# A build-time list scheduler for the order of all instructions, a variable share of exps on VectorE, and the last sums in two jobs

## The chip, the cores and the metric

The kernel runs on one core of a Trainium2 chip. The metric is the time of one execution in device microseconds (us). A run is given as the median of its executions; the span of a profile is the time from the first to the last instruction of the one execution that was profiled. PE is the matmul engine, ACT the engine of activation functions, DVE the vector engine, POOL and SP are the two others. PEld is PE's loading of weights, which overlaps its matmuls (5 us of the trace below, from 555.00, hold 4.58 us of PE and 1.36 of PEld).

## The reference

Two independent parts share one output of 2048 x 1024. Part A is attention with 32 heads of 16 dimensions and one common key and value; part B is linear attention with a softmax feature map.

```python
q = (x @ wq).reshape(B, S, 32, 16)           # part A, S = 2048
k, v = x @ wk, x @ wv                        # one key and value for all heads
p = softmax(einsum("bhqd,bkd->bhqk", q, k) * 16 ** -0.5)
a = einsum("bhqk,bkd->bhqd", p, v) @ wo

pq, pk = q2 @ w_phi, k2 @ w_phi              # part B, per head
phi = concat(softmax(pq), softmax(-pq))      # the same for k
kv, z = phi_k.T @ v2, phi_k.sum(0)
b = ((phi_q @ kv) / (phi_q @ z + 1e-6)) @ wo2
```

Part A has 32 x 2048 x 2048 exps. The kernel cuts them into 2048 score tiles of 128 keys by 512 queries. That is nearly all of the work outside PE.

## The kernel before

The head dimension is only 16, padded to 32, so a score matmul uses 32 rows of the array, and up to four of them run side by side on four row groups. The trace of the kernel before shows it: three score matmuls start together at 506.88 us, within 0.01 us, and the next job starts 0.32 us after them; four start at 507.75 us, and the next job 0.34 us after. Each product with the values uses 32 columns, again four side by side: four start at 506.13 us, and the next four 0.22 us later.

ACT takes exps in groups of three and two tiles, out of five PSUM banks used in turn (3 + 2). One bank collects the products with the values. The last two banks, 6 and 7, serve everything else: projections, all of part B, and the score tiles whose exp DVE computes from integer bits. In the kernel before, the order was written by hand. Each step emits one score group and its exp, then whatever is due, up to a budget of PE time; what is left of the budget is filled with matmuls by zero ("fills"), which are meant to keep PE's clock up (in the runs below the clock was 0.784 to 0.808 without them and 0.873 to 0.898 with those of the changed kernel).

```python
def misc(self):                               # the two shared banks, in turn
    b = self.MISC[self.misc_n % len(self.MISC)]
    self.misc_n += 1
    return b

def d_unit(self, busy):                       # one score tile for DVE
    ...
    bank = self.misc()
    self.add("pe", lambda pe: self.score(pe, bank, sc, kap, g), cost=0.1, ...)
    o = self.Z[:, p, h, :]
    self.add("dve", lambda v: v.tensor_scalar(out=o, in0=ps[:, bank, :], scalar1=self.Z1, scalar2=self.Z0, op0=ALU.mult, op1=ALU.add), ...)
    if h:
        self.d_fields(k // 2)                 # two bit operations on a pair of tiles
    self.d_mul(k // 2 - 1 + h, 1 - h)         # two multiplications on a pair

self.layout([0] + [3, 2] * 15 + [0])          # quads of tiles on DVE, for each 512 queries of four heads: 75 in all
...
for i, (n0, size, b0) in enumerate(gs):       # plan()
    self.pe_used = over
    self.qk(n0, size, b0)
    self.expo(n0, size, b0)
    ...                                       # a DVE tile, and products with V, if due
    budget = self.EXP_US[gs[i - 1][1]] if i else 0.5
    while H and H[0][0] <= i:                 # projections, part B: by due step
        if self.pe_used > budget and H[0][0] > i - 5 and i > 12:
            break
        heapq.heappop(H)[2]()
    if i >= 13 and self.open:
        ...
        while self.pe_used + 0.216 <= budget:
            self.fill()
```

Each engine is given its instructions in this order. A semaphore holds each one until its inputs and its buffers are ready, and the timeline below shows what that does to those behind it (a score matmul waited 1.58 us for DVE at 563.67 us).

## Time and profile before

The time before was 1070.84 us (median of 2 runs, 1068.35 to 1073.33).

| | before |
|---|---|
| span of the profile | 1069.9 us |
| busy: PE, ACT, DVE | 81%, 79%, 72% |
| ACT idle for score matmuls | 207.0 us |
| mean granted clock | 0.868 |
| filling matmuls recorded | 493 |
| score tiles on ACT, on DVE | 1748, 300 |

The first fence has lines of the profile page of the kernel before: the busy time of each engine; the granted clock of PE in 40 slices of the span, in tenths; the chain of waits that ended last; and four groups of instructions. A group has line, engine, operation and shapes, then busy us and mean ns of one, then the idle time of the engine just before them and what ended most of it. L1441 is the exps on ACT, L1421 the score matmuls, L1479 the first DVE step of a DVE tile, L1256 the fills.

```profile
PE 870.9 (81%) x6933; PEld 248.0 (23%) x6933; DVE 771.3 (72%) x1401; ACT 846.3 (79%) x768; POOL 16.5 (2%) x44
PEclk9899898989986989698987888969789688988998
...
DVE 35%; PE 32%; ACT 25%; DMA 3%; SPq 2%; issue 1%; DVEq 0%; POOL 0%; POOLq 0%
...
L1441 ACT ACTIVATE f_PT<-f_ps 128x1536 bf16<-128x1536 f32 (+1 forms) x699 | 816.7, 1277 | 209.2 <-PE f_ps L1421 207.0
L1421 PE MATMUL f_ps<-f_QA,f_KR 32*128 32x512 bf16 x2048 | 331.5, 421 | 109.1 <-ACT f_PT L1441 58.7
L1479 DVE TENSOR_SCALAR f_Z<-f_ps 128x512 int16<-128x512 f32 x300 | 205.1, 684 | 120.4 <-PE f_ps L1421 120.2
...
L1256 PE MATMUL f_ps<-f_ones,f_zero 128*128 128x512 bf16 x493 | 166.8, 417 | 1.9 <-POOL f_zero L1280 1.3
```

No engine is full. ACT waits for scores, and DVE waits for scores too. The next fence, from the table of windows of the kernel before, shows one episode: us, then busy us of PE, PEld, DVE, ACT and POOL, then the granted clock, DMA share and GB/s.

```profile
555.00:560.00 5.00, 4.58 (x38) 1.36 (x36) 3.95 (x8) 4.29 (x4) 0.00 (x0) 1.00 0.00 0
560.00:565.00 5.00, 3.19 (x30) 0.92 (x28) 4.90 (x9) 3.28 (x3) 0.00 (x0) 1.00 0.08 30
565.00:570.00 5.00, 1.96 (x19) 0.86 (x19) 4.93 (x12) 1.66 (x2) 0.00 (x0) 0.52 0.10 28
570.00:575.00 5.00, 3.94 (x12) 1.06 (x13) 2.20 (x4) 0.82 (x1) 0.00 (x0) 0.50 0.00 0
575.00:580.00 5.00, 3.69 (x34) 0.91 (x36) 2.65 (x5) 3.87 (x4) 0.00 (x0) 0.84 0.00 0
```

DVE is full from 560 to 570, PE is half idle, the clock falls to 0.50, and ACT does 0.82 us of work in 5. The timeline of the kernel before shows why PE is idle: the brackets give the idle time before an instruction and what ended it.

```profile
563.67 0.39 PE L1421 MATMUL f_ps<-f_QA,f_KR 32*128 32x512 bf16 x1 [1.58 <-DVE f_outA L1267]
564.27 0.40 PE L1808 MATMUL f_ps<-f_ident,f_o_sb 128*128 128x128 bf16 x4 [0.21 <-DVE f_Z L1479]
...
566.86 0.60 PE L1421 MATMUL f_ps<-f_QA,f_KR 32*128 32x512 bf16 x1 [1.87 <-DVE f_Z L1479]
...
568.39 0.38 PE L1785 MATMUL f_ps<-f_Zc,f_pT 128*128 128x4 bf16 x8 [0.93 <-DVE f_Z L1479]
...
569.79 1.02 ACT L1441 ACTIVATE f_PT<-f_ps 128x1024 bf16<-128x1024 f32 x1 [3.31 <-PE f_ps L1421]
...
572.09 3.68 PE L1574 MATMUL f_ps<-f_wo_pad,f_On 128*128 128x512 bf16 x8
...
576.13 4.62 ACT L1441 ACTIVATE f_PT<-f_ps 128x1536 bf16<-128x1536 f32 x4 [5.32 <-PE f_ps L1421]
```

A score tile for DVE, or a job of part B (L1808, L1785), stands in PE's queue, waits for one of the two shared banks, and everything behind it waits too, the scores for ACT among them. The last two lines show a second loss: the hand-written order put the eight matmuls of an output projection before the next scores. PE is busy with them, but at half clock they take 3.68 us (eight of the same line took 2.13 us at full clock, from 283.89 us), and ACT has waited 5.32 us when the scores come.

### The profile page before, as it was taken

How to read it: one execution, taken by the hardware profiler on the slowest of the kernel's cores; microseconds unless marked ns; L12 is line 12 of the kernel's file. 1: busy time of each engine (PE TensorE's matmuls, PEld its weight loads, DVE VectorE, ACT ScalarE, POOL GpSimd, SP SyncE). 2: the span in 40 equal slices, each digit the busy share in tenths (PEclk: the TensorE clock that was granted, in tenths of full speed). 3: DMA queues.
4: the chain of work that ended last, by engine and by line, in shares of the span. 5: the costliest groups of instructions: out<-in, count | busy, mean ns of one | idle time of the engine just before them, and what ended most of it. 6: DMA issues, size and time to landing. Idle time of an engine off the chain costs nothing.

```text
span 1069.9 us, 16576 instructions
## 1 busy us (share of the span) xinstructions
PE 870.9 (81%) x6933; PEld 248.0 (23%) x6933; DVE 771.3 (72%) x1401; ACT 846.3 (79%) x768; POOL 16.5 (2%) x44
## 2 busy tenths in 40 slices
PE   8897888888777879788796888888778788887885
PEld 2222222222221212122221222222122122222221
DVE  4577679778676887777857877787776787878712
ACT  5889787988866978688874888969778578877994
POOL 4000000000000000001000000000000000000000
PEclk9899898989986989698987888969789688988998
DMA  6700010000001000000000100111000010011110
GB/s 119 159 7 6 6 7 6 4 4 6 6 12 17 5 6 7 6 1 6 6 6 11 17 6 6 6 26 6 1 6 6 31 16 6 6 26 6 7 25 23
DMA packets 40667, 17.06 MB, mean 16 GB/s; under 512 B 32580, under 2 KB 38212, under 8 KB 40584
## 3 DMA queue, kind: packets, MB, share of 16 engines
q1 hardware_dynamic: 40584, 15.93, 12.0%
q8 instruction: 55, 0.90, 0.4%
q14 instruction: 28, 0.23, 0.1%
HBM read 3.19 MB, written 4.19 MB: 7 GB/s over the span
## 4 chain that ended last, share of the span: by engine, by line
DVE 35%; PE 32%; ACT 25%; DMA 3%; SPq 2%; issue 1%; DVEq 0%; POOL 0%; POOLq 0%
ACT f_PT L1441 23%; PE f_ps L1421 10%; DVE f_Z L1479 9%; DVE f_C L1501 7%; PE f_ps L1454 5%; PE f_ps L1256 4%; PE f_ps L1394 3%; DVE f_phi L1727 3%; DVE f_U L1489 3%; DVE f_ssum L1719 3%; PE f_ps L1515 2%; DVE f_E L1491 2%; ACT f_epn L1713 2%; PE f_ps L1574 2%; DMA f_denS<-f_denS 2%; PE f_ps L1676 2%
## 5 line engine op out<-in xcount | busy, mean ns | idle before, releaser
L1441 ACT ACTIVATE f_PT<-f_ps 128x1536 bf16<-128x1536 f32 (+1 forms) x699 | 816.7, 1277 | 209.2 <-PE f_ps L1421 207.0
L1421 PE MATMUL f_ps<-f_QA,f_KR 32*128 32x512 bf16 x2048 | 331.5, 421 | 109.1 <-ACT f_PT L1441 58.7
L1479 DVE TENSOR_SCALAR f_Z<-f_ps 128x512 int16<-128x512 f32 x300 | 205.1, 684 | 120.4 <-PE f_ps L1421 120.2
L1454 PE MATMUL f_ps<-f_PT,f_VA 128*32 128x512 bf16 x1748 | 170.7, 426 | 17.4 <-DVE f_accS L1267 15.9
L1256 PE MATMUL f_ps<-f_ones,f_zero 128*128 128x512 bf16 x493 | 166.8, 417 | 1.9 <-POOL f_zero L1280 1.3
L1421 PEld LDWEIGHTS f_ps<-f_QA,f_KR 32*128 32x128 bf16 x2048 | 73.3, 92 | 398.0 <-ACT f_PT L1441 244.2
L1501 DVE TENSOR_TENSOR f_C<-f_Z,f_U 128x1024 f16<-128x1024 f16 x150 | 102.7, 684 | 0.0
L1501 DVE TENSOR_TENSOR f_C<-f_C,f_U 128x1024 f16<-128x1024 f16 x150 | 102.1, 680 | 0.0
L1489 DVE TENSOR_SCALAR f_U<-f_Z 128x1024 int16<-128x1024 int16 x150 | 64.1, 427 | 5.2
L1491 DVE TENSOR_SCALAR f_E<-f_Z 128x1024 int16<-128x1024 int16 x150 | 63.0, 420 | 0.0
L1454 PEld LDWEIGHTS f_ps<-f_PT,f_VA 128*32 128x32 bf16 x1748 | 36.8, 97 | 106.8 <-issue 69.2
L1559 DVE TENSOR_TENSOR f_On<-f_accS,f_denS 128x512 bf16<-128x512 f32 x31 | 21.3, 689 | 51.9 <-DMA f_denS<-f_denS 51.9
L1256 PEld LDWEIGHTS f_ps<-f_ones,f_zero 128*128 128x128 bf16 x493 | 38.0, 100 | 87.1 <-issue 68.3
L1394 PE MATMUL f_ps<-f_AxT,f_wq_pad 128*128 128x512 bf16 x128 | 47.0, 506 | 13.6 <-DVE f_Z L1479 12.4
L1727 DVE TENSOR_TENSOR f_phi<-f_epn,f_rs 128x1024 bf16<-128x1024 f32 x32 | 39.2, 1224 | 1.1
L1676 PE MATMUL f_ps<-f_BxT,f_Bw 128*128 128x512 bf16 x128 | 37.3, 419 | 2.7 <-DVE f_Z L1479 2.0
L1719 DVE TENSOR_REDUCE f_ssum<-f_epn 128x64 f32<-128x1024 f32 x32 | 38.6, 1207 | 0.0
L1267 DVE CAST f_QA<-f_ps 128x512 bf16<-128x512 f32 x32 | 22.0, 688 | 21.6 <-PE f_ps L1394 21.5
L1713 ACT ACTIVATE f_epn<-f_ps 128x512 f32<-128x512 f32 x64 | 35.7, 633 | 1.2 <-PE f_ps L1704 1.2
L1574 PE MATMUL f_ps<-f_wo_pad,f_On 128*128 128x512 bf16 x96 | 31.3, 459 | 5.4 <-ACT f_epn L1713 1.9
L1515 PE MATMUL f_ps<-f_E,f_VK 128*32 128x512 f16 x300 | 32.6, 425 | 0.0
L1515 PE MATMUL f_ps<-f_Z,f_VK 128*32 128x512 f16 x300 | 32.1, 419 | 0.0
(90 smaller groups left out, 462.0 us busy)
## 6 DMA issues: line engine op xcount, KB each, us to landing
f_denS<-f_denS SPq DMA_DIRECT2D x124, 30.0 KB, 3.1
out_dram<-f_outB SPq DMA_DIRECT2D x4, 512.0 KB, 3.4
f_denC<-f_accS SPq DMA_DIRECT2D x124, 2.0 KB, 1.7
f_denS<-f_denC SPq DMA_DIRECT2D x124, 2.0 KB, 1.7
f_Bw<-in_B_wqkv_dram SPq DMA_DIRECT2D x1, 1536.0 KB, 8.0
out_dram<-f_outA SPq DMA_DIRECT2D x6, 256.0 KB, 2.6
f_outB<-in_A_wq_dram SPq DMA_DIRECT2D x1, 512.0 KB, 4.4
f_Bwo<-in_B_wo_dram SPq DMA_DIRECT2D x1, 512.0 KB, 7.8
```

Source lines behind the costliest of these rows:

```text
L1256: mm = pe.matmul(out, lhsT=self.zero, rhs=rhs, start=start, stop=start)
L1394: mm = pe.matmul(ps[:, bank, :], lhsT=self.wq_pad[:, dc, a, :], rhs=xT[:, dc, qc * 512:(qc + 1) * 512], start=(dc == 0), stop=(dc == 3))
L1421: return pe.matmul(self.ps[:, bank, :], lhsT=self.KR[32 * g:32 * g + 32, kap * 128:(kap + 1) * 128], rhs=self.QA[32 * g:32 * g + 32, sc % ...
L1441: self.add("act", lambda a: a.activation(out=PT[:, sl[0]:sl[0] + size, :], in_=ps[:, b0:b0 + size, :], func=ACT.Exp), reads=[("PS", b0 + i ...
L1454: mm = pe.matmul(ps[32 * g:32 * g + 32, bank, :], lhsT=VA[:, kap, :], rhs=PT[:, slots[g], :], start=start, stop=stop, tile_position=(0, 32 ...
L1479: self.add("dve", lambda v: v.tensor_scalar(out=o, in0=ps[:, bank, :], scalar1=self.Z1, scalar2=self.Z0, op0=ALU.mult, op1=ALU.add), reads ...
L1489: self.add("dve", lambda v: v.tensor_scalar(out=U, in0=Z, scalar1=0x3ff, scalar2=0x3c00, op0=ALU.bitwise_and, op1=ALU.bitwise_or), reads=z ...
L1491: self.add("dve", lambda v: v.tensor_scalar(out=E, in0=Z, scalar1=0x7c00, scalar2=None, op0=ALU.bitwise_and), reads=zk, writes=[("E", p)])
L1501: self.add("dve", lambda v: v.tensor_tensor(out=C, in0=a, in1=U, op=ALU.mult), reads=rd + [("U", r)], writes=[("C0", p), ("C", p)] if h == ...
L1515: mm = pe.matmul(ps[32 * g:32 * g + 32, bank, :], lhsT=self.VK[:, k, kap, :], rhs=terms[k][:, p, h, :], start=start and k == 0, stop=stop ...
L1719: self.add("dve", lambda v: v.tensor_reduce(out=ssum[:, r, :], in_=epn[:, r, :, :].rearrange("p a (h f) -> p (a h) f", h=32), axis=AX.X, o ...
L1727: self.add("dve", lambda g: g.tensor_tensor(out=o, in0=i0, in1=i1, op=ALU.mult), reads=[("epn", r), ("epn2", r), ("rs", r)], writes=[("phi ...
```

## The change

The change replaces the hand-written steps by jobs with a length, an engine and a list of what must come first. A list scheduler runs a model of the engines at build time. On each engine it picks, among the jobs whose inputs and banks the model says are ready, the one with the best priority; on PE, a job that uses the array in the same tiling as the job before has a bonus. Banks are named at that moment, the one that frees first. PE is held free when a job would delay the next score group (`spare`). Fills go into planned gaps when PE's busy time over the last 3.4 us of the model is below 80%. Which tiles DVE takes is decided on the way, from DVE's load. The final sums of part B put numerator and denominator into one bank and go in two halves. The arithmetic of the result is otherwise the same. The core of the diff, with cuts marked and some lines joined:

```diff
-    def misc(self):
-        b = self.MISC[self.misc_n % len(self.MISC)]
-        self.misc_n += 1
-        return b
+    def ready(self, j):                       # (cut) the latest of its inputs in the model,
+        ...                                   # and of the banks it needs:
+        if j.nb:
+            fr = sorted(max(self.tr.get(("PS", b), (0.0,))[0], 0.0) + self.SEM for b in self.free)
+            if len(fr) < j.nb:
+                return None
+            t = max(t, fr[j.nb - 1])
+        return t
+    def active(self, t, win=3.4):
+        while self.pe_hist and self.pe_hist[0][1] < t - win:
+            self.pe_hist.pop(0)
+        return sum(min(b, t) - max(a, t - win) for a, b in self.pe_hist) / win
 ...
-        self.layout([0] + [3, 2] * 15 + [0])
-        for i, (n0, size, b0) in enumerate(gs):
-            ...
+    def dq_ok(self):                          # may DVE take another tile?
+        if self.dbusy > 3.2 or self.dz_out or (...):
+            return False
+        return self.dn % 4 != 0 or self.dve_quad() is not None
+    def run(self):
+        while True:
+            ...
+                lo = min(o[0] for o in opts)
+                now = [o for o in opts if o[0] <= max(lo, te) + 0.02]
+                if eng == "pe":
+                    now = self.spare(now, opts)
+                s, j = min(now, key=lambda o: (self.rank(o), o[1].seq))
+            ...
+            if j.eng == "pe" and self.open:
+                te = self.te["pe"]
+                if s - te > 0.36 and te > 14 and self.active(te) < self.ACTIVE:   # ACTIVE = 0.80
+                    n = min(int((s - te - 0.12) / 0.216), 4)
+                    self.issue(_Job(("fill", len(self.log)), "pe", 0.216 * n, lambda: self.fill(n), ...), te)
+                    continue
 ...
-            for G in range(8):
-                mm = pe.matmul(ps[:, bd, 4 * G:4 * G + 4], lhsT=pT[:, r, G, :], rhs=Zc[:, G, :], start=True, stop=True)
-            for G in range(8):
-                mm = pe.matmul(ps[:, bn, 64 * G:64 * G + 64], lhsT=pT[:, r, G, :], rhs=KV[:, G, :], start=True, stop=True)
+            for i in range(4):                # twice per row tile: h = 0, 1
+                mm = pe.matmul(ps[:, bank, 68 * i:68 * i + 68], lhsT=pT[:, r, 4 * h + i, :], rhs=KVZ[:, 4 * h + i, :], start=True, stop=True)
```

## The prediction

> **What bounds the kernel now.** No engine is full: PE is busy 81%, ACT 79%, DVE 72% of 1069.9 us (busy time by engine). The chain of waits is shared: DVE 35%, PE 32%, ACT 25%. ACT's exps (the groups) take 816.7 us for 1748 of the 2048 score tiles, 0.467 us a tile; ACT's idle time is almost all one wait, 207 us for score matmuls. Those come late because PE takes instructions in order and stands behind a matmul whose PSUM bank DVE has not emptied (waits of score matmuls for DVE f_Z, f_o_sb, f_outA, f_kvS; at 564-575 us of the timeline). DVE in turn idles 120 us before f_Z, waiting for scores. So the fixed order passes stalls round a loop.
>
> The rest of the loss is the clock. Of 5-us windows after 20 us, 116 with full clock show ACT 94% busy, 31 with clock at most 0.6 show 53%, 52 between show 67%. Mean granted clock is 0.868; with cold at 0.5 that is 26% of the time cold. Cold stretches follow windows in which DVE is full (4.9 of 5 us) and PE stalls.[...]
>
> **What the change does.** It keeps nearly all arithmetic. It orders jobs by modelled readiness, so that PE should not queue behind an unready bank, reserves room for the next score group, picks the bank that frees first, and fills PE only when its recent activity is below 80%. Part B's last sums go in two halves with numerator and denominator in one bank: 8 matmuls a row tile instead of 16, one bank at a time instead of two (that wait costs PE about 12 us now)[...]. DVE's share of exps becomes dynamic; I expect it to rise from 300 to 330-420 tiles.
>
> **Cost.** A DVE tile occupies about 1.55 us: steps in the timeline are 0.60 for f_Z, half of 0.34+0.34 and of 0.60+0.60 per pair. DVE's other work is 234 us busy, about 215 occupied (estimate). ACT has about 30 us of other work, 12 us before its first exp, 12 us of tail. The last 60 us have DVE nearly idle; a dynamic share can use that. With ACT useful 94% and DVE 86%: (0.94T-40)/0.467 + (0.86T-215)/1.55 = 2048 gives T = 885 us (estimate); full use about 830. PE, without most of its 167 us of fills, has some 700 us of work when warm (estimate), so it is no bound unless cold.
>
> Prediction: **885 us**, 840 to 960. Faster by over 2%: 0.94; within 2%: 0.03; slower by over 2%: 0.03.
>
> **What would show it right.** ACT busy at least 88%; its wait for score matmuls below 100 us; clock at least 0.93; score matmuls' waits for DVE f_Z and f_o_sb mostly gone; fewer than 493 fills; more than 300 tiles on DVE; DVE above 80%. Wrong: clock still near 0.87, or PE's waits for DVE as large as now.
>
> **What would make it wrong.** The order is fixed at build time from a model with full clock and fixed DMA landings. One cold spell or late DMA puts all engines off the plan, and a tight order has less slack; with PE about 80% loaded it recovers slowly. Less filling may make the clock drop more often. Then 950-1000. If the plan holds everywhere, 840.

For the clock, the trace of the kernel before shows this: its records are 1.00 or 0.50 and nothing else, 0.50 for 284.8 us in all; in the 5 us before a fall, DVE was busy for at least 4.85 us at 22 of the 39 falls, so not before all of them.

## The result, and the profile after

The changed kernel took 915.99 us (median of 2 runs, 913.39 to 918.59) against 1070.84; the ratio is 0.8554, with a 95% interval of 0.8419 to 0.8689. A ratio is the mean time of one kernel's fast runs over that of the other's of the same rounds, so it is not quite the ratio of the medians. A later batch with more runs gave 919.52 us and 0.8545 (0.8489 to 0.8601). The predicted 885 us was 3.4% too low; 916 us lies inside the stated range.

The page of the changed kernel, with the lines that answer to those above (L1606 is the exps, L1551 the scores, L1697 the first DVE step, L1365 the fills):

```profile
PE 798.6 (88%) x6535; PEld 240.4 (26%) x6602; DVE 812.3 (89%) x1581; ACT 819.3 (90%) x751; POOL 17.0 (2%) x47
PEclk9697699999799997899889998777778898999798
...
DVE 54%; PE 31%; ACT 13%; issue 1%; DMA 0%; SPq 0%; DVEq 0%; POOL 0%; POOLq 0%
...
L1606 ACT ACTIVATE f_PT<-f_ps 128x1536 bf16<-128x1536 f32 (+1 forms) x682 | 790.6, 1268 | 74.7 <-PE f_ps L1551 71.9
L1551 PE MATMUL f_ps<-f_QA,f_KR 32*128 32x512 bf16 x2048 | 363.0, 417 | 65.6 <-ACT f_PT L1606 49.1
L1697 DVE TENSOR_SCALAR f_Z<-f_ps 128x512 int16<-128x512 f32 x344 | 231.8, 688 | 36.5 <-PE f_ps L1551 36.1
...
L1365 PE MATMUL f_ps<-f_ones,f_zero 128*128 128x512 bf16 x178 | 66.2, 453 | 1.9 <-POOL f_zero L1384 1.3
```

The span fell by 158.7 us. ACT accounts for all of it by definition (busy plus idle is the span): its busy time fell by 27.0 us, of which the 44 tiles that moved to DVE are 44 x 0.467 = 20.5, and its idle time fell from 223.6 to 91.9 us, by 131.7 us. So five sixths of the gain is ACT no longer standing idle for scores.

The clock hardly moved: 0.868 before, 0.889 after. But the kernel lost less while it was low. In windows of 5 us after the first 20 us, ACT was busy like this:

| granted clock in the window | before: windows, ACT busy | after: windows, ACT busy |
|---|---|---|
| full (1.00) | 116, 94% | 114, 97% |
| 0.60 to 0.94 | 52, 67% | 35, 82% |
| below 0.60 | 31, 53% | 26, 76% |

(Eight windows before and three after, between these bounds, are left out, and so are the last 15 us before.)

The next two fences, from the windows and the timeline of the changed kernel, show a fall of the clock in it.

```profile
170.00:175.00 5.00, 4.80 (x45) 1.55 (x42) 4.72 (x9) 5.00 (x5) 0.00 (x0) 1.00 0.00 0
175.00:180.00 5.00, 3.93 (x63) 1.63 (x61) 5.00 (x10) 5.00 (x7) 0.00 (x0) 0.94 0.00 0
180.00:185.00 5.00, 5.00 (x38) 1.19 (x36) 4.17 (x9) 3.62 (x5) 0.00 (x0) 0.72 0.03 5
```

```profile
176.47 0.40 PE L1961 MATMUL f_ps<-f_wphi,f_qkT 128*128 128x128 bf16 x4
176.83 0.39 PE L1551 MATMUL f_ps<-f_QA,f_KR 32*128 32x512 bf16 x3
177.71 0.43 PE L1551 MATMUL f_ps<-f_QA,f_KR 32*128 32x512 bf16 x3 [0.48 <-DVE f_Z L1697]
178.07 0.40 PE L1648 MATMUL f_ps<-f_PT,f_VA 128*32 128x512 bf16 x4
178.90 0.37 PE L2003 MATMUL f_ps<-f_vaug,f_phi 128*32 128x17 bf16 x32 [0.43 <-DVE f_Z L1697]
179.44 1.48 PE L1944 MATMUL f_ps<-f_Bw,f_BxT 128*128 128x512 bf16 x3 [0.16 <-issue]
```

PE does not stand still for long here (the waits in brackets are 0.48 us at most), and ACT is busy all 5 us. The clock falls at 179.4 us all the same. What runs before it is small in the array: scores on 32 of 128 rows, and 32 matmuls of 17 columns of data on 32 array columns.

That led to a measure that the profile does not print. In the records of the clock in the two traces, every change lies on a grid of 3.413 us. For each such window I added up the streaming time of the matmuls in the trace, each weighted by its active rows x columns / 16384 (128 x 128 is the largest tile in the trace). Streaming time is an estimate from the steps from one matmul to the next in the trace of the kernel before: these are 0.427 us for 512 columns at half clock and 0.216 us at full clock, and at full clock 0.056 us for 128 and 0.029 us for 64 (medians over matmuls of one line on the whole array). I counted 0.427 us for 512 columns at half clock, half of that, 0.213 us, at full clock, and other matmuls in proportion to their columns; with 0.216 us in place of 0.213 the edge given next is 0.39 as well. In the window before the fall at 179.4 us, 38% of the time had a matmul streaming, but the array share was 0.26. In the two traces no window at full clock with an array share above 0.39 was followed by half clock. This is a correlation; the second batch below tests it.

### The profile page after: what moved, and what is told of

Same layout as the page of the kernel before. It is cut to its first block, busy times and chain, and to the rows that moved or that the text cites. A ratio compares the mean times of both kernels' runs of the same rounds, so it can differ in the third digit from the quotient of the medians.

```text
span 911.2 us, 16012 instructions
## 1 busy us (share of the span) xinstructions
PE 798.6 (88%) x6535; PEld 240.4 (26%) x6602; DVE 812.3 (89%) x1581; ACT 819.3 (90%) x751; POOL 17.0 (2%) x47
## 4 chain that ended last, share of the span: by engine, by line
DVE 54%; PE 31%; ACT 13%; issue 1%; DMA 0%; SPq 0%; DVEq 0%; POOL 0%; POOLq 0%
DVE f_Z L1697 15%; ACT f_PT L1606 12%; PE f_ps L1551 11%; DVE f_C L1721 7%; DVE f_C L1723 6%; PE f_ps L1648 5%; DVE f_U L1717 4%; PE f_ps L1746 4%; DVE f_E L1719 3%; PE f_ps L1365 3%; DVE f_phi L1991 2%; DVE f_ssum L1976 2%; PE f_ps L1929 2%; DVE f_QA L1371 1%; DVE f_qkT L1371 1%
## 5 line engine op out<-in xcount | busy, mean ns | idle before, releaser
L1606 ACT ACTIVATE f_PT<-f_ps 128x1536 bf16<-128x1536 f32 (+1 forms) x682 | 790.6, 1268 | 74.7 <-PE f_ps L1551 71.9
L1551 PE MATMUL f_ps<-f_QA,f_KR 32*128 32x512 bf16 x2048 | 363.0, 417 | 65.6 <-ACT f_PT L1606 49.1
L1697 DVE TENSOR_SCALAR f_Z<-f_ps 128x512 int16<-128x512 f32 x344 | 231.8, 688 | 36.5 <-PE f_ps L1551 36.1
L1648 PE MATMUL f_ps<-f_PT,f_VA 128*32 128x512 bf16 x1704 | 185.4, 425 | 3.3 <-DVE f_accS L1371 3.0
L1551 PEld LDWEIGHTS f_ps<-f_QA,f_KR 32*128 32x128 bf16 x2048 | 82.3, 92 | 331.5 <-ACT f_PT L1606 186.2
L1723 DVE TENSOR_TENSOR f_C<-f_C,f_U 128x1024 f16<-128x1024 f16 x172 | 117.5, 686 | 0.0
L1721 DVE TENSOR_TENSOR f_C<-f_Z,f_U 128x1024 f16<-128x1024 f16 x172 | 117.2, 687 | 0.0
L1365 PE MATMUL f_ps<-f_ones,f_zero 128*128 128x512 bf16 x178 | 66.2, 453 | 1.9 <-POOL f_zero L1384 1.3
L1541 PE MATMUL f_ps<-f_AxT,f_wq_pad 128*128 128x512 bf16 x109 | 32.4, 415 | 4.5 <-issue 2.4
L1746 PE MATMUL f_ps<-f_C,f_VK 128*32 128x512 f16 x344 | 35.7, 405 | 0.0
L1371 DVE CAST f_qkT<-f_ps 128x512 bf16<-128x512 f32 x32 | 22.1, 690 | 6.9 <-PE f_ps L1929 6.9
```

The source lines that it names most:

```text
L1365: mm = pe.matmul(out, lhsT=self.zero, rhs=rhs, start=start, stop=start)
L1371: self.add("dve", lambda v: v.tensor_copy(out=out, in_=in_), reads=reads, writes=writes)
L1551: return pe.matmul(self.ps[:, bank, :], lhsT=self.KR[32 * g:32 * g + 32, kap * 128:(kap + 1) * 128], rhs=self.QA[32 * g:32 * g + 32, sc % ...
L1606: self.add("act", lambda a: a.activation(out=PT[:, sl[0]:sl[0] + size, :], in_=ps[:, b0:b0 + size, :], func=ACT.Exp), reads=[("PS", b0 + i ...
L1648: mm = pe.matmul(ps[32 * g:32 * g + 32, bank, :], lhsT=w, rhs=PT[:, slots[g], :], start=start, stop=stop, tile_position=(0, 32 * g))
L1721: self.job(("dL", pair), "dve", 0.60, step(0.6, lambda v: v.tensor_tensor(out=C, in0=Zf, in1=Uf, op=ALU.mult), reads=zk + [("U", r)], writ ...
```

## The experiments

The theory on the order: the gain comes from PE no longer standing behind unready banks, not from the greater share of DVE. The rivals are the share itself and the split of the sums. The theory on what remains: the clock follows the array share of each window, so the planner's measure (PE busy with anything) fills in the wrong amount. Its rivals are that PE's busy time is what counts, and that chip and plan drifting apart makes the clock fall. All kernels gave correct results. Times are medians of the fast runs; four of the kernels had one or two runs more than 1.5% above their fastest, and those are left out. The ratio is to the kernel before in the same batch, whose median was 1071.62, 1072.24 and 1072.46 us in the three batches; that of the run with 296 tiles also holds runs that are marked slow (see there). The clock is the range over the fast runs; ACT's wait for scores is from the one profiled run. The list is made anew for each edit, so a run can differ from the changed kernel in more than its edit: where the share was not capped, the list runs have 340 to 348 tiles on DVE.

| run | us | ratio (95%) | clock | ACT's wait, us |
|---|---|---|---|---|
| changed, again | 919.52 | 0.8545 (0.8489 to 0.8601) | 0.873 to 0.898 | 78.4 |
| fixed order, 344 tiles on DVE | 1096.2 | 1.0214 (1.0174 to 1.0253) | 0.840 to 0.850 | 249.6 |
| fixed order, no tiles on DVE | 1023.39 | 0.9555 (0.9517 to 0.9593) | 0.976 to 0.979 | 38.4 |
| list, 296 tiles on DVE | 930.13 | 0.8721 (0.8687 to 0.8755) | 0.882 to 0.901 | 61.8 |
| list, sums joined | 902.10 | 0.8408 (0.8366 to 0.8449) | 0.905 to 0.918 | 58.7 |
| list, no reservation | 912.49 | 0.8514 (0.8464 to 0.8563) | 0.914 to 0.920 | (slow run) |
| list, no fills | 969.56 | 0.9051 (0.8983 to 0.9119) | 0.784 to 0.808 | 114.5 |
| list, fills on 32 x 32 | 976.71 | 0.9098 (0.9017 to 0.9180) | 0.783 to 0.802 | 125.4 |
| list, fills in every gap | 897.59 | 0.8395 (0.8355 to 0.8434) | 0.944 to 0.954 | 48.0 |
| list, fills by array share | 889.65 | 0.8318 (0.8272 to 0.8365) | 0.954 to 0.968 | 39.4 |
| the same, also without a gap | 879.05 | 0.8199 (0.8147 to 0.8251) | 0.977 to 0.988 | 38.4 |
| the same, sums joined | 878.46 | 0.8190 (0.8163 to 0.8217) | 0.985 to 0.991 | 29.1 |

### The changed kernel again

> The changed kernel once more, as the control of this batch: 916 us as in the first two runs, within 1%; ACT 90%, DVE 89% busy, mean granted clock near 0.889.

Measured: 919.52 us in the median of four runs. Each run has its own clock, and the times follow it: 923.35 us at 0.873, 922.36 at 0.878, 916.69 at 0.887, 911.38 at 0.898. The spread of 1.3% (0.7% in the kernel before) is thus mostly the clock's, and small differences against this kernel have to be read with the clock beside them.

### The share of DVE in the fixed order

```diff
-        self.layout([0] + [3, 2] * 15 + [0])
+        self.layout([0] + ([3] * 6 + [2]) * 4 + [3, 3] + [0])      # 344 tiles
```

> The kernel before, in its fixed order, with 344 score tiles on DVE instead of 300 (what the changed kernel has). Theory 'the order is what counts': more DVE work in an order that already makes PE stand behind DVE gives nothing, 1060 to 1110 us, with the clock no higher than 0.87. Rival 'the share is what counts': ACT has 44 tiles less, 44 x 0.467 = 21 us less of exps, so 1050 us or less, and most of the 155 us in the extreme form of the rival.

Measured: 1096.2 us, 2.1% slower. The same share that the changed kernel has costs time in the old order. The page of this run shows where: ACT has less to do and waits longer, and score matmuls wait longer for DVE (46.1 us in all before, counted over the PE rows of the table of waits; 60.5 us here; 12.5 us in the changed kernel).

```profile
L1441 ACT ACTIVATE f_PT<-f_ps 128x1536 bf16<-128x1536 f32 (+1 forms) x682 | 799.7, 1264 | 251.9 <-PE f_ps L1421 249.6
```

```diff
-        self.layout([0] + [3, 2] * 15 + [0])
+        self.layout([0] * 32)                                      # no tile on DVE
```

> The kernel before, in its fixed order, with no score tiles on DVE at all: all 2048 on ACT. ACT then has 2048 x 0.467 = 956 us of exps and 30 us of other work. Theory 'in the fixed order DVE's tiles cost PE as much by stalls and half clock as they save ACT': DVE is less than half busy, PE hardly stands behind it, clock above 0.95, and the time is 1010 to 1070 us, so no slower than before. Rival 'the kernel before was short of exp throughput': 300 tiles more on ACT cost 140 us, 1150 us or more.

Measured: 1023.39 us, 4.5% faster than the kernel before. In the fixed order, DVE's 300 tiles cost more than they saved. The page of this run:

```profile
PE 906.9 (89%) x6877; PEld 263.2 (26%) x6877; DVE 299.6 (29%) x501; ACT 966.1 (95%) x888; POOL 15.6 (2%) x44
PEclk9999999999998999999997999999999997999998
...
L1441 ACT ACTIVATE f_PT<-f_ps 128x1536 bf16<-128x1536 f32 (+1 forms) x819 | 940.3, 1378 | 40.1 <-PE f_ps L1421 38.4
...
L1256 PE MATMUL f_ps<-f_ones,f_zero 128*128 128x512 bf16 x1037 | 307.8, 388 | 1.9 <-POOL f_zero L1280 1.3
```

ACT took on 123.6 us of exps (940.3 against 816.7) and lost 168.6 us of waiting for scores. Score matmuls waited 0.4 us for DVE in all. One thing is not separated: the budget rule also let in 1037 fills instead of 493, so part of the higher clock may be due to fills, not only to the missing stalls.

### The share of DVE in the list

```diff
-            if sc < 32 and ("qa", sc) in self.issued and ...
+            if sc < 32 and self.dt[sc] < ([0] + [3, 2] * 15 + [0])[sc] and ("qa", sc) in self.issued and ...
```

> The changed kernel with the DVE share of each head capped at that of the kernel before (296 to 300 tiles in all). Theory 'the order is what counts': ACT has 44 to 48 tiles more, 22 us more of exps, and is about 97% busy while the clock is full, so 925 to 945 us. Rival 'the share is what counts': back to 1000 us or more. The clock should stay near 0.88 by either.

Measured: 930.13 us. With the list and nearly the old share (296 tiles), the ratio is 0.8721, so the list without the greater share gives 12.8%. That ratio is what the runs of 936.31, 934.56 and 936.20 us give, and two of these are marked slow, as the fastest run took 920.85. The three fast runs have a mean of 928.5 us; over 1072.7, the mean of the kernel before in this batch, that is 0.866, a gain of 13.4%. The greater share is worth about 10 us between the means of the fast runs (918.5 against 928.5), and this is not clear of the noise: the runs overlap (911.38 to 923.35 against 920.85 to 934.56). The 48 tiles are 48 x 0.467 = 22 us of exps. So the theory holds: the order carries the gain, and a greater share, which costs time in the old order, adds little to it.

### The split of the last sums

The experiment puts the sums back into one job of 16 matmuls that needs both free banks at once.

```diff
-            for h in range(2):
-                job(("s4", st, h), "pe", 0.25, ..., nb=1, ...)
+            job(("s4", st, 0), "pe", 0.60, ..., nb=2, ...)
```

> The changed kernel with the final sums of part B done as before: one job per row tile that needs both free PSUM banks at once, 16 matmuls, one set of DVE steps. Theory 'the split is a minor part': within 1% of the changed kernel (16 jobs, at most about 1 us of PE wait each[...]). Rival 'two banks at once were a main stall': at least 15 us slower.

(In the two traces the DVE steps of these sums take 1.23 us a row tile in one job, before, and 1.69 us in two halves, after: the mean times of the three steps.)

Measured: 902.10 us, not slower but faster than the changed kernel of the same batch, by 1.9% and so outside both expectations, with intervals of the ratio that do not overlap. The clock was higher too, 0.905 to 0.918 in the fast runs. Whether the split costs time was tested again with the clock held up (last run below): there both forms agree, 878.46 against 879.05 us. So the split gives nothing that shows, and the 1.9% here goes with the clock: it is gone when the clock is held up. Why this order had the better clock is open.

### The reservation for the next scores

```diff
                 if eng == "pe":
-                    now = self.spare(now, opts)
+                    pass
```

> The changed kernel without the rule that holds PE back when a job would delay the next group of scores; everything else of the list stays. If that rule is what frees ACT: ACT waits longer for scores (72 to 80 us now) and the time is 15 us or more longer. If readiness of the banks alone does it: within 1% of the changed kernel, 910 to 930 us.

Measured: 912.49 us in the two fast runs, ratio 0.8514, the same as the changed kernel within its interval. The reservation is not what carries the gain of 155 us. But its clock was higher (0.914 and 0.920 against 0.873 to 0.898), so a smaller worth of the reservation may be hidden, and the run does not settle it. Its profile fell in a slow run (926.0 us, with 84.6 us of ACT waiting for scores), so ACT's wait is not compared. What is left of the list is the choice by readiness and priority, the bank that frees first, the bonus for the same tiling on PE, and the time at which part B is let in (its jobs are released from 54 to 750 us of the model; its last output projection starts at 788 us in the changed kernel, at 1008 us before). These were not taken apart.

### Fills and the clock

```diff
-    ACTIVE = 0.80
+    ACTIVE = 0.0
```

> The changed kernel with no filling matmuls after the first ten. If the filling that is left (178 matmuls in the trace) still holds the clock up, the mean clock falls below 0.87 and the time rises by 15 us or more; if the fills only cost PE time, the time stays or falls and the clock stays near 0.889.

Measured: 969.56 us, clock 0.784 to 0.808. The fills that the change left in were worth 50 us. So removing 315 of the 493 recorded fills was no saving in itself.

```diff
-                mm = pe.matmul(out, lhsT=self.zero, rhs=rhs, start=start, stop=start)
+                if start: ...                                       # the first ten stay as they were
+                else:
+                    mm = pe.matmul(out[0:32], lhsT=self.zero[0:32, 0:32], rhs=rhs[0:32], start=False, stop=False, tile_position=(0, 0))
```

> The changed kernel with every fill as long as before but on a 32 x 32 corner of the array. Theory 'the clock follows the share of the array in use' (in the two traces, no full-clock window of 3.4 us with matmul streaming time weighted by rows x columns / 16384 above 0.39 was followed by half clock): it behaves like the kernel without fills, clock and time within 1% of it. Rival 'the clock follows the time in which PE is busy with anything': it behaves like the changed kernel, 0.885 to 0.895 and 916 us.

Measured: 976.71 us, clock 0.783 to 0.802. The page of this run shows that the fills are there and take about as long as those of the changed kernel (68.3 us in all, against 66.2 with the first ten), on a sixteenth of the array (the first ten, on the whole array, form a group of their own):

```profile
PE 891.0 (91%) x6602; PEld 246.5 (25%) x6602; DVE 818.6 (84%) x1581; ACT 825.5 (85%) x751; POOL 16.4 (2%) x47
...
L1368 PE MATMUL f_ps<-f_ones,f_zero 32*32 32x512 bf16 x168 | 68.3, 494 | 0.1
```

PE is busy 91%, more than in the changed kernel, and the clock is as low as with no fills at all (0.783 to 0.802 against 0.784 to 0.808). So in these runs the clock does not go with PE's busy time: about as long fills on the whole array went with 0.873 to 0.898, in the changed kernel.

The planner was then given the array share as its measure. Each job has a weight: its streaming time times its share of the array.

```diff
-            self.pe_hist.append((start, start + dur))
+            self.pe_hist.append((start, start + dur, self.work(j) / dur))
...
-        return sum(min(b, t) - max(a, t - win) for a, b in self.pe_hist) / win
+        return sum((min(b, t) - max(a, t - win)) * w for a, b, w in self.pe_hist) / win
+    WORK = dict(pv=0.213, dpv=0.64, dq=0.053, pk=0.853, pq=0.853, op=0.853, pp=0.75, pva=0.107, bp=0.853, bv=0.853, s8=0.853, pqk=0.213, kv=0.057, s2=0.427, s4=0.113, s6=0.213)
...
-    ACTIVE = 0.80
+    ACTIVE = 0.55
```

> The changed kernel, but the planner's activity is the streaming time weighted by the share of the array (threshold 0.55) instead of PE's busy time (0.80); fills still only go into planned gaps of over 0.36 us; about 390 fills. Theory of the array share: half-clock windows fall by more than half, mean clock 0.93 or more, 885 to 905 us. Rival 'stalls from plan and chip drifting apart make the clock fall, whatever the fills': clock within 0.01 of 0.889, time within 1% of 916 or longer.

Measured: 889.65 us, clock 0.954 to 0.968. Windows of 3.413 us at half clock fell from 59 of 266 in the first profile of the changed kernel to 16 of 258. The order is as tight as before, so drift between plan and chip is not what lowered the clock most of the time.

```diff
+                if te > 14 and j.name[0] != "qk" and self.active(te) < 0.45:
+                    self.issue(_Job(("fill", len(self.log)), "pe", 0.432, lambda: self.fill(2), ...), te)
+                    continue
```

> As the last, and where the weighted activity is below 0.45 two fills go in even without a planned gap (not ahead of a score group that is due); about 490 fills. Theory of the array share: clock 0.95 or more, 870 to 895 us. Rival 'PE has no room': PE gets fuller, ACT waits longer for scores, 916 us or more.

Measured: 879.05 us, clock 0.977 to 0.988, half-clock windows 11 of 256. The page of this run:

```profile
PE 799.2 (91%) x6838; PEld 250.5 (29%) x6838; DVE 806.9 (92%) x1581; ACT 816.4 (93%) x751; POOL 19.2 (2%) x47
...
DVE 73%; PE 18%; ACT 6%; DMA 1%; issue 1%; SPq 0%; DVEq 0%; POOL 0%; POOLq 0%
...
L1616 ACT ACTIVATE f_PT<-f_ps 128x1536 bf16<-128x1536 f32 (+1 forms) x682 | 786.6, 1269 | 41.7 <-PE f_ps L1561 38.4
...
L1375 PE MATMUL f_ps<-f_ones,f_zero 128*128 128x512 bf16 x414 | 130.4, 402 | 2.2 <-POOL f_zero L1394 1.3
```

This kernel has the same 344 tiles on DVE and 236 more fills than the changed one (414 against 178 recorded), and is faster than both kernels. The chain that ended last is now 73% DVE.

```diff
-    ACTIVE = 0.80
+    ACTIVE = 9.0          # the old measure, never above it: fill every planned gap
```

> The changed kernel with fills in every planned gap of over 0.36 us, no threshold at all (about 440 fills, against about 390 by the array share and about 200 as changed). If only the amount of filling in gaps counts: 880 to 900 us and a clock of 0.96 or more, like the run with fills by array share. If filling where the array share is low is what counts and fills elsewhere delay PE: 900 to 920 us.

Measured: 897.59 us, clock 0.944 to 0.954. It falls at the edge between the two expectations. Filling every gap gives most of the gain; the array-share rule with gaps alone was 8 us faster with fewer fills (332 recorded against 373), but the two intervals of the ratio touch, so that difference is unclear. The forced fills are clear of it.

> The forced filling by array share together with the final sums of part B in one job over two banks. The joined sums were 1.6% faster under the original filling, at a higher clock (0.905 against 0.873). If that gain was only the clock's luck: within 1% of 879 us, on either side. If the split itself costs time: 865 us or less.

Its edit is those of the two runs in its name together. Measured: 878.46 us in six runs, the same as with the split.

### The measure over all profiles

Over the 14 profiles (both kernels and the twelve runs; this count is by window and needs no equal times), 2510 windows at full clock had an array share of 0.42 or more, and none was followed by half clock; of 267 between 0.36 and 0.42, 42 were; of 165 between 0.30 and 0.36, 139; of 149 below 0.30, 148. (27 of these windows lie before the first record of the clock and are counted as full.) The edge of 0.39 from the first two traces held in the other twelve: there the highest share before a fall was 0.40. Without the weight, by the fraction of the window in which any matmul streamed, there is no such edge: of 854 windows between 0.42 and 0.60, 181 were followed by half clock. Other measures do worse too. In the 3064 full-clock windows from the first record on, 329 before a fall, the best single threshold on the array share misjudges 47 windows; on the time with any matmul streaming 181, on PE's busy time 216, on a weight by columns alone 246, by rows alone 260, and on the longest pause between matmuls 313. On the way back, all 195 half-clock windows with an array share of 0.78 or more were followed by full clock, and 4 of 305 below 0.66.

The longest pause between matmuls in the windows before the 25 falls of the changed kernel was 0.29 to 1.47 us. Transposes are counted in full in the array share; when the windows are counted without them, the best threshold misjudges 121 full-clock windows in place of 47. The fills multiply by an operand of zeros: 414 recorded ones went with a clock of 0.979 (the profile with fills also without a gap), and only the first ten with 0.795 (the one without fills).

## Why the prediction was right, and where not

- **The mechanism was right.** PE stood behind unready banks, and the list ended most of it: over all matmuls (the PE rows of the table of waits), PE's waits for DVE fell from 118.6 us to 37.8. ACT's wait for scores fell from 207.0 to 71.9 us (forecast below 100). PE's waits of score matmuls fell from 19.2 to 6.3 us for f_Z and from 10.1 to 1.9 us for f_o_sb. At the weight loads the sum for f_Z hardly fell (28.1 to 26.4 us), but in 58 waits of at most 1.1 us instead of 28 of at most 2.2. Two experiments confirm it from both sides: more DVE tiles in the fixed order were slower by 2.1%, none at all faster by 4.5%.
- **The busy shares were right.** ACT 90% (forecast at least 88%), DVE 89% (above 80%), 344 tiles on DVE (330 to 420), 178 fills (fewer than 493).
- **The step that was off is the clock**: "clock at least 0.93". It was 0.889, and 0.873 to 0.898 in the next four runs, so that of the prediction's two signs of being wrong one, "clock still near 0.87", came true. The prediction had cold stretches follow stalls of PE, so it expected them to go with the stalls. Before the change that was a fair reading: in the windows before its 39 falls of the clock, the longest pause between matmuls was 1.49 us in the median (0.57 to 3.15). After the change there were still 25 falls, with a longest pause of 0.80 us in the median; PE was working, but on small parts of the array (an array share of at most 0.37 in these windows), and two thirds of the fills were gone.
- **The size follows from that step.** The estimate took ACT useful for 94% of T. With the same sum, the changed kernel has (790.6 + 40) / 911.2 = 91%, and DVE has (344 x 1.55 + 215) / 911.2 = 82% against the 86% assumed. With the clock held up by fills it has (786.6 + 40) / 876.8 = 94%, and DVE has (344 x 1.55 + 215) / 876.8 = 85%: 879 us measured against the 885 predicted. Holding the clock up gave 40 us, which is more than the 31 us between 885 and 916. That the first result lies in the range in spite of the clock is owed to the width of the range. (At full use the prediction's sum gives 816 us, not "about 830"; nothing else rests on that.)
- **Of the named dangers** one came true, "less filling may make the clock drop more often": without any fills the time was 969.56 us. "A tight order has less slack" did not show: in the windows below 0.60 of the clock ACT was still 76% busy, against 53% in the fixed order.
- **The split of the sums was overrated.** The trace of before does show 12.5 us of PE waiting at these sums for f_Z, but joining the sums again under the list cost nothing that shows.

Left open: how much of the gain is the choice by readiness, the choice of bank, the bonus for the same tiling or the other place of part B; what the reservation is worth at an equal clock; and how much of the clock of the run without DVE tiles is due to its extra fills.

## What to carry to other kernels

When engines that take instructions in order share a few buffers, first ask who stands behind whom: here the helper's tiles were worth less than nothing until the order was changed, and removing the help was the quick test that showed it. When PE's clock matters, judge each window of 3.4 us by streaming time times the share of the array, not by PE's busy time: in the 14 profiles none of 2510 full-clock windows at 0.42 or more was followed by half clock, and 148 of 149 below 0.30 were; fills on 32 x 32 of the array left PE 91% busy at a clock of 0.793. And do not count filler matmuls as pure waste: here the ones still left were worth 50 us, and more of them, better placed, 40 us more.
